# Output blocks of nine products laid over two pairs of steps in one order

## The chip, the cores and the metric

The kernel runs on one core of a Trainium2 chip. The metric is device time in microseconds (us) from start to end of one execution. Three runs of the kernel before gave 1628.75, 1627.30 and 1627.44 us; the median is 1627.44 us.

Engines are named as in the profile: PE (TensorE, matmuls; PEld are its weight loads), DVE (VectorE), ACT (ScalarE), POOL (GpSimd) and SP (SyncE, which issues most of the transfers; SPq is its queue).

## The reference, cut to what matters

```python
# xn = layernorm(x), x: 2048 tokens x 512
q, k, v = split(xn @ wqkv)                  # 32 heads of 16
p = softmax(q @ k.T / 4)                    # per head, 2048 x 2048
s = concat_heads(p @ v) @ wo
h = layernorm(xn)
u = gelu(h.T @ w1 + b1)                     # MLP over the tokens, F = 1792
y = (u @ w2 + b2).T
out = x + s * silu(y)
```

The output is 2048 x 512 in f32. Products that are not attention products are made of three matmuls each: operands are split into a high and a low part (h, l), and hh, hl and lh are summed.

## The kernel before, in words

Heads are worked in 16 pairs. For one pair of heads the kernel goes twice over the keys, once for each half of the queries (1024 rows, a "span"). One step `t` is one block of 128 keys against a span of queries, for both heads of a pair. It makes four score tiles of 128 x 512 (`score`, line 987: a matmul into a bank of PSUM named `sc`, then an exponential on ACT into a tile `prob`, line 992). Two steps later `values` (line 1003) multiplies the four tiles with the values and adds them up in a bank named `av`; this is eight matmul records, called an av set below.

The softmax needs the maximum of each row beforehand. So 22 steps (`LEAD`) ahead of the scores the same product is made the other way round for steps `u` (`max_of`, line 532, banks named `mx`), and DVE takes the maximum of each 128 x 512 tile (line 536). After 16 steps `max_rows` is called. It gives two parts, which are put in a list `pieces`: `first_` reduces the 16 steps' maxima and turns one block of 32 x 32, `last` turns three more blocks (line 548), and then POOL splits the result in two (lines 559 and 94) and issues four transfers on its own queue (line 98) that write it as two extra rows into the query tile of either head (first both rows of head a = 0, then both of a = 1). The scores of that span, six steps on, multiply 50 rows instead of 48 and so read these rows.

The loop over `s` goes by pairs of steps, from 0 to 534; steps s and s + 1 of the maxima run beside steps s - 22 and s - 21 of the scores and s - 24 and s - 23 of the av sets. One pair of steps holds 8 maxima, 8 scores and 2 av sets. Heads a = 0 and a = 1 sit in rows 0 to 63 and 64 to 127 of the PE array, so that two matmuls, one for each half, run beside each other: this is a slot. Into these slots goes other work (`Fill`, written D): products of the mixer MLP up to s = 456, and after that the output product, which `rest` makes in 14 blocks (`PARTS`) of nine products: three groups of eight heads times hh, lh, hl. Each product is cut into its upper and lower 64 rows, so a block is 18 half products. They add up in one bank that `hold` takes out of the four `sc` banks; while it is held the scores rotate over three.

`ORDERS` (line 1117) gives the order within one pair of steps. It has one string for each half of the PE array, and each letter is a maximum (m), a score (s) or a half product (D); the two numbers behind are the places at which an av set goes ahead of the slot. At the first of them `piece()` runs one of the waiting pieces; at both `run_later()` runs what has been put off (`after(n, f)` puts `f` off by n such calls). `halves` takes n products from the fill and `count` says how many: for a block of nine it gives 4 in the first pair of steps and 5 in the second. `lead`, the half of the array that has its D at the front of its string, changes after each pair. At the end of a pair the functions that end a block (`then`) are called: `part` copies the bank to a tile with ACT (line 910), the bank goes back, and POOL multiplies and adds (lines 913, 914) before SP stores (line 921).

When a span of a pair of heads is done, `put_away` copies the av bank out (line 723) and stores it. After the last pair of a group `invert` puts off a function `two`: DVE takes reciprocals of the row sums (line 751), and SP stores them to DRAM (line 752). `two` waits in `pieces` as well. At the start of a pair of steps `divisions` looks whether the reciprocals were stored, and `divide` then loads numerators and reciprocals (lines 775, 779). Later POOL multiplies (line 786), casts to the high part (line 798) and subtracts for the low part (line 94). The last of these divisions feeds the first block of the final stage (s >= 512, line 1188), of which the first two products need the high part and the third the low part.

Of the kernel before, what the change touches and what calls it, by code (L numbers as in the profile page):

```python
# [21 lines left out]
def tile_attention_token_mixer(ctx, tc, x, wqkv, wo, w1, b1, w2, b2, out):  # L22
    nc = tc.nc
    P = 128
    S, D = x.shape
# [11 lines left out]
    LEAD = 22  # L37
# [132 lines left out]
    with (  # L170
# [172 lines left out]
        two = first(0, range(2, 4), True)  # L343
# [64 lines left out]
        for c in range(NC):  # L408
# [20 lines left out]
            for n, (part, g) in enumerate(order):  # L429
                m = slice(g * P, (g + 1) * P)  # L430
# [75 lines left out]
    now = [0]  # L506
# [420 lines left out]
    def load_second():  # L927

        b = next((b for b in unkept if b >= PARTS), min(unkept))
        unkept.remove(b)  # L930
        i = b - NB // 2
        while not held or len(held) < NB // 8:
            held.append(big.tile([P, S], F32, name="big"))
        ys[b] = held[i // 4][:, i % 4 * 512 : i % 4 * 512 + 512]
        nc.sync.dma_start(ys[b], y_d[b] if b < PARTS else xv[:, b, :])
# [145 lines left out]
    def take(n, each):  # L1081

        nonlocal open_, done
        got = 0
        while open_ and (got < n or fill.peek() and len(fill.peek()) == 2):
            x = fill.next()
            if x is False:
                open_ = False
            elif x is None:
                break  # L1090
            elif len(x) == 2:
                def then(empty, back):
                    empty()
                    back()

                each(None, lambda x=x: then(*x))
                if fill.peek() is None:
                    fill.next()
                    break
            else:  # L1100
                each(x, None)
                got += 1
        done += got
# [98 lines left out]
    def items(s, a):  # L1202
# [7 lines left out]
                sc.append(lambda t=t, i=i, at=(ps_mx, "mx") if a and s >= NU else (ps_sc, "sc"): score(t, i % 2, a, *at))  # L1210
        return mx, sc

    take(FIRST, whole)
    after(5, lambda: load_v(0))
    if NP > 1:
# [4 lines left out]
    def piece():  # L1220
        if pieces:
            pieces.pop(0)()
            return True
        return False

    lead = 0
    for s in range(0, total + 1, 2):
        t = s - LEAD
        now[0] = s
        if s >= NU or t < 0:  # L1230
            run_later()
        if done >= n_fill // 2 + 3 * NF:
            divisions()
        if s >= NU - SPP + LEAD and unkept:
            load_second()
        if s == NU:

            ps_sc.free += ps_mx.free
            ps_mx.free = ps_sc.free
        heads = [items(s, a) for a in range(2)]  # L1240
        if s < NU and t >= 0:
            steady[0] = True
            one, two, then = halves(lead, count())
            made = [dict(D=part, m=heads[a][0], s=heads[a][1]) for part, a in ((one, lead), (two, 1 - lead))]
            first, second, *places = order(len(one), new_block[0])
            if one:
                lead = 1 - lead
            for i, kinds in enumerate((*zip(first, second), "")):
                if i in places:

                    if i == places[0]:
                        piece()
                    now[0] = s + places.index(i)
                    if now[0] >= LEAD + 2:
                        values(now[0] - LEAD - 2)
                    run_later()
                for of, kind in zip(made, kinds):
                    if of[kind]:
                        of[kind].pop(0)()
            for f in then:  # L1260
                f()
        elif s < NU:

            for i in range(4):
                for a in range(2):
                    max_of(s + i // 2, i % 2, a, *first_banks[n_max % 4])
                    n_max += 1
                end = i == 3 and s + 2 == LEAD
                some = []
                take(EARLY[n_max // 2 % len(EARLY)], lambda *x: some.append(x))  # L1270
                for x in some:
                    lanes(*x, stop=end and x is some[-1])
                if end:
                    keep_half()
                if i == 1:
                    now[0] = s + 1
                    run_later()
        else:


            for i in range(2):

                a_half(*(heads[a][1][2 * i : 2 * i + 2] for a in range(2)), i == 0 or s >= NU + 2 * (PARTS - NB // 2))
                if not piece() and asides and s < total - 2:
                    asides.pop(0)()
                for v in range(t - 2, t + i):
                    if (v, 0, 0) in prob:
                        values(v)
                if i == 0:
                    now[0] = s + 1  # L1290
                    run_later()
            if s == NU + 4:
                load_last_w()
            for _ in in_halves[:2]:
                load_half()
            if s == total - 6:
                split_last_w()
# [124 lines left out]
```

## Time and profile before

| | before |
|---|---|
| median of three runs | 1627.44 us (1627.30 to 1628.75) |
| the profiled execution's own time | 1627.72 us |
| its span, first to last instruction | 1625.8 us |
| granted clock of TensorE | 0.999 |
| PE busy | 1618.6 us (100%) |
| DVE busy | 1421.3 us (87%) |
| ACT busy | 1195.8 us (74%) |
| POOL busy | 559.9 us (34%) |
| the 14 output blocks | about 1402 to 1556 us of the span |

All times in the rows are microseconds from the first instruction of the span. In a row of the timeline stand the start, the length, the engine, the line, the operation, the tiles (written <- read), their shapes, the count of merged instructions, and in square brackets the idle time before it and who ended it. Matmul records overlap: a record of 0.39 us does not keep the next matmul on the same half of the array from starting 0.23 us after it. So starts are compared here, and the busy share of PE says little.

### The profile page before, as it was taken

To read this page: it belongs to the slowest core of one execution; us is meant where nothing else is said; L and a number is where in the kernel's file an instruction comes from. 1 tells how busy PE (TensorE), PEld (TensorE's weight loads), DVE (VectorE), ACT (ScalarE), POOL (GpSimd) and SP (SyncE) were. 2 spreads that over 40 slices of the span, in tenths; PEclk is the share of its full clock that TensorE was granted. 3 is DMA by queue.
4 is the path that set the end of the run, shared out by engine and by line. 5 is a ranking of instruction groups with operands and counts; after the bars stand their busy time and mean duration, and the time that the engine had idled before them with its cause. 6 is when DMAs were issued, how large, how long until landed. Compare 5 with 4: busy or idle time off the path is not lost.

```text
span 1625.8 us, 31245 instructions
## 1 busy us (share of the span) xinstructions
PE 1618.6 (100%) x11937; PEld 876.6 (54%) x11937; DVE 1421.3 (87%) x2492; ACT 1195.8 (74%) x2312; POOL 559.9 (34%) x665
## 2 busy tenths in 40 slices
PE   9999999999999999999999999999999999999998
PEld 7888854554555544544545545545545445444444
DVE  7665999999999999999999999999999999999956
ACT  3333477777777777778877877777777778888885
POOL 1224844342244432342333332322322233632440
PEclk9999999999999999999999999999999999999999
DMA  7478441514142141926151512314151615353365
GB/s 228 177 249 206 114 93 41 95 43 73 41 71 71 32 79 34 244 66 109 39 86 38 86 61 44 76 25 69 38 85 38 112 39 94 120 98 119 115 186 194
DMA packets 152466, 155.60 MB, mean 96 GB/s; under 512 B 51628, under 2 KB 110252, under 8 KB 149244
## 3 DMA queue, kind: packets, MB, share of 16 engines
q1 hardware_dynamic: 147900, 152.85, 38.6%
q8 instruction: 94, 1.54, 0.4%
q0 software_dynamic: 4416, 0.75, 0.4%
q14 instruction: 56, 0.46, 0.1%
HBM read 101.86 MB, written 50.58 MB: 94 GB/s over the span
## 4 chain that ended last, share of the span: by engine, by line
PE 99%; DMA 0%; DVE 0%; ACT 0%; SPq 0%; issue 0%; POOL 0%; DVEq 0%
PE av L1003 31%; PE dn L1144 24%; PE sc L987 16%; PE mx L532 15%; PE sc L435 3%; PE dn L670 3%; PE mx L435 2%; PE av L435 1%; PE sc L101 0%; PE sc L103 0%; PE sc L102 0%; PE mx L987 0%; DMA wl<-in_A_wqkv_dram 0%; PE mx L101 0%; PE mx L103 0%; PE mx L102 0%
## 5 line engine op out<-in xcount | busy, mean ns | idle before, releaser
L536 DVE TENSOR_REDUCE mxp<-mx 128x1 f32<-128x512 f32 x2026 | 1251.8, 682 | 118.3 <-PE mx L532 100.3
L992 ACT ACTIVATE prob<-sc 128x512 f32<-128x512 f32 x2004 | 1039.3, 607 | 284.6 <-PE mx L532 126.8
L532 PE MATMUL mx<-big 48*128 48x512 f32 x2026 | 773.7, 419 | 0.0
L987 PE MATMUL sc<-big 50*128 50x512 f32 x2004 | 739.8, 412 | 0.1
L1003 PE MATMUL av<-prob,vp 128*32 128x512 f32 x4096 | 545.5, 604 | 0.2 <-DVE ev L721 0.2
L1144 PE MATMUL dn<-hu,wh 64*128 64x512 f32 x1520 | 507.4, 404 | 0.0
L987 PEld LDWEIGHTS sc<-big 50*128 50x128 f32 x2004 | 354.2, 186 | 238.8 <-ACT prob L992 210.6
L532 PEld LDWEIGHTS mx<-big 48*128 48x128 f32 x2026 | 358.0, 185 | 195.4 <-DVE mxp L536 178.2
L1144 PEld LDWEIGHTS dn<-hu,wh 64*128 64x128 f32 x1520 | 271.9, 184 | 73.6 <-issue 49.5
L1144 PE MATMUL dn<-hu,wl 64*128 64x512 f32 x762 | 302.3, 397 | 0.0
L1003 PEld LDWEIGHTS av<-prob,vp 128*32 128x32 f32 x4096 | 80.9, 108 | 180.3 <-issue 168.0
L94 POOL TENSOR_TENSOR wl<-raw,wh 128x512 fp32r<-128x512 f32 x124 | 150.7, 1217 | 60.0 <-ACT wh L166 26.6
L1144 PEld LDWEIGHTS dn<-hu,wl 64*128 64x128 f32 x762 | 140.5, 184 | 12.1
L164 POOL CAST wh<-raw 128x512 fp32r<-128x512 f32 x104 | 60.4, 580 | 192.1 <-PE mx L532 79.5
L559 POOL CAST m<-f 16x128 fp32r<-16x128 f32 x32 | 9.0, 280 | 303.6 <-DVE f L548 303.6
L98 POOL DMA_DIRECT2D big<-m x128 | 66.2, 525 | 2.7 <-PE mx L987 2.7
L620 POOL TENSOR_TENSOR sq<-u 128x512 f32<-128x512 f32 x11 | 11.4, 1041 | 133.0 <-ACT u L614 132.9
L1144 PE MATMUL dn<-wh,hu 64*128 64x512 f32 x168 | 55.1, 393 | 0.0
L707 POOL TENSOR_SCALAR t<-t 128x512 f32<-128x512 f32 x16 | 23.8, 1488 | 83.7 <-ACT t L704 83.7
L435 PE MATMUL sc<-xt,big 128*128 128x512 f32 x184 | 44.3, 389 | 0.0
L94 POOL TENSOR_TENSOR hu<-hx,hu 128x512 fp32r<-128x512 f32 x16 | 20.4, 1292 | 68.4 <-ACT hu L278 68.4
L670 PE MATMUL dn<-hu,wh 64*128 64x512 f32 x128 | 42.3, 392 | 0.0
(233 smaller groups left out, 1212.1 us busy)
## 6 DMA issues: line engine op xcount, KB each, us to landing
raw<-in_B_w_dram SPq DMA_DIRECT2D x104, 256.0 KB
big<-k_d SPq DMA_DIRECT2D x96, 128.0 KB
big<-q_d SPq DMA_DIRECT2D x96, 128.0 KB
q_d<-sg SPq DMA_DIRECT2D x16, 512.0 KB
k_d<-sg SPq DMA_DIRECT2D x16, 512.0 KB
num_d<-ev SPq DMA_DIRECT2D x30, 256.0 KB
u_d<-uo SPq DMA_DIRECT2D x14, 512.0 KB
hu<-u_d SPq DMA_DIRECT2D x14, 512.0 KB
```

The lines of the kernel that those rows point to most:

```text
L94: eng.tensor_tensor(out=o, in0=a, in1=b.bitcast(F32), op=OP.subtract)
L98: queue.dma_start(dst.bitcast(F32), src.bitcast(F32))
L164: nc.gpsimd.tensor_copy(whs[n][:, :m, :], raws[n][:, :m, :])
L435: nc.tensor.matmul(ps, w[part][:, kd, m], xt[kd][:, z, :], start=w is wh and z == 0 and kd == 0, stop=w is wl and kd == ND - 1,)
L532: nc.tensor.matmul(ps, q[o : o + 48, r * P : (r + 1) * P], k[o : o + 48, c * 512 : (c + 1) * 512], start=True, stop=True,)
L536: nc.vector.tensor_reduce(mxp[u // 16][:, a, r % 8, c : c + 1], ps, axis=AX.X, op=OP.max)
L670: nc.tensor.matmul(ps, w(slice(0, 64)), m(slice(0, 64)), start=first, stop=last)
L707: nc.gpsimd.tensor_scalar(t, t, 1.0, None, op0=OP.add)
L987: nc.tensor.matmul(ps, ks[p][o : o + 50, kb * P : (kb + 1) * P], qs[p][o : o + 50, at : at + 512], start=True, stop=True,)
L992: nc.scalar.activation(e, ps, AF.Exp, scale=scale)
L1003: nc.tensor.matmul(av[32 * j : 32 * j + 32, :], vps[p][:, kb, 16 * a : 16 * a + 32], prob.pop((t, a, c)), start=kb == 0, stop=kb == NB - 1,)
L1144: made.append(lambda r=r, start=first and a == lead, stop=last and a != lead: nc.tensor.matmul(ps, w(r), m(r), start=start, stop=stop,))
```

## The change

A new table `WIDE` holds one order for a whole block of nine products, over two pairs of steps (25 slots, the same letters in number as before: 18 D, 16 m, 16 s). `both_pairs` emits it whenever a pair with s divisible by four starts a new block of nine; the loop's next pair then emits nothing but what stands behind the slots. This holds for all 14 blocks, s = 456, 460, ..., 508. The differences in what is emitted:

- Each half of the array has its nine D in one burst of its own: slots 3 to 11 on the half of `lead`, slots 15 to 23 on the other. `lead` no longer changes.
- The bank of the block is taken at slot 3 and given back at slot 23 (`then` is called behind the last D, not at the end of the pair).
- The four av sets stand ahead of slots 2, 12, 15 and 24, each followed by `run_later()`.
- `piece()` is called ahead of slots 12 and 24, where before it was called at the first av set of each pair.
- `keep` (divisions and loads) of the second pair is called ahead of slot 15.

```diff
+    WIDE = ("mssDDDDDDDDDsmsmsmmssmsmm", "smmsmsmsmsmsmmsDDDDDDDDDs", 2, 12, 15, 24)
+
+    def both_pairs(s, keep):
+
+        heads = [[x + y for x, y in zip(items(s, a), items(s + 2, a))] for a in (lead, 1 - lead)]
+        made = [dict(m=mx, s=sc) for mx, sc in heads]
+        first, second, *places = WIDE
+        one, two, then = [], [], []
+        for i, kinds in enumerate((*zip(first, second), "")):
+            if i in places:
+                n = places.index(i)
+                if n == 2:
+                    keep(s + 2)
+                if n % 2:
+                    piece()
+                now[0] = s + n
+                values(now[0] - LEAD - 2)
+                run_later()
+            if "D" in kinds and not one and not two:
+                one, two, then = halves(lead, 9)
+                assert len(one) == len(two) == 9
+            for of, rows, kind in zip(made, (one, two), kinds):
+                (rows if kind == "D" else of[kind]).pop(0)()
+            if then and not two:
+                then.pop()()
...
     for s in range(0, total + 1, 2):
         t = s - LEAD
-        now[0] = s
+        now[0] = max(s, now[0])
         if s >= NU or t < 0:
             run_later()
-        if done >= n_fill // 2 + 3 * NF:
-            divisions()
-        if s >= NU - SPP + LEAD and unkept:
-            load_second()
+        if s != second_pair:
+            keep(s)
...
         heads = [items(s, a) for a in range(2)]
-        if s < NU and t >= 0:
+        if s == second_pair:
+            pass
+        elif s < NU - 2 and s % 4 == 0 and done >= n_fill and count() == 4 and new_block[0]:
+            both_pairs(s, keep)
+            second_pair = s + 2
+        elif s < NU and t >= 0:
```

Three places of the order are shown. The first is PE where one output block ends and the next begins; `dn` is the block's bank (its number names the block), `wh`/`wl` and `hu` are operands of the output product, `sc` and `mx` are score and maximum. Before:

```order
L1144 MATMUL dn_20656<-wh_20154,hu_19919 128x512
L987 MATMUL sc_20816<-big_1481,big_1482 128x512
L1144 MATMUL dn_20656<-wl_20155,hu_19919 128x512
L532 MATMUL mx_20821<-big_1372,big_1371 128x512
L1144 MATMUL dn_20656<-wh_20154,hu_19919 128x512
L1144 MATMUL dn_20827<-wh_19981,hu_10896 128x512
L987 MATMUL sc_20829<-big_1481,big_1482 128x512
L1144 MATMUL dn_20827<-wl_19982,hu_10896 128x512
L532 MATMUL mx_20834<-big_1372,big_1371 128x512
```

PE at such a place after the change:

```order
L1144 MATMUL dn_20531<-wh_20154,hu_19919 128x512
L1003 MATMUL av_20333<-prob_20544,vp_18318 32x512
L1003 MATMUL av_20333<-prob_20553,vp_18318 32x512
L1003 MATMUL av_20333<-prob_20579,vp_18318 32x512
L1003 MATMUL av_20333<-prob_20592,vp_18318 32x512
L532 MATMUL mx_20649<-big_1372,big_1371 128x512
L987 MATMUL sc_20652<-big_1481,big_1482 128x512
L532 MATMUL mx_20658<-big_1372,big_1371 128x512
L987 MATMUL sc_20661<-big_1481,big_1482 128x512
```

Before, the next block's D follows the old block's last D in the same burst, so the next bank is taken at once; now an av set, three slots and another av set stand between.

The second place is DVE in blocks s = 496 to 508, from the last turned maxima (line 548) to the end of the stage; line 751 is the last reciprocal, `mxp` the maxima. Before:

```order
L548 STREAM_TRANSPOSE f<-neg_141 32x32 x3
L536 TENSOR_REDUCE mxp<-mx 128x1 x32
L751 RECIPROCAL d<-d 96x64
L536 TENSOR_REDUCE mxp<-mx 128x1 x22
L94 TENSOR_TENSOR hu<-sq,hu 96x512
```

DVE after the change:

```order
L548 STREAM_TRANSPOSE f<-neg_141 32x32 x3
L536 TENSOR_REDUCE mxp<-mx 128x1 x32
L751 RECIPROCAL d<-d 96x64
L536 TENSOR_REDUCE mxp<-mx 128x1 x17
L94 TENSOR_TENSOR hu<-sq,hu 96x512
```

The reciprocal, and the turned maxima 32 maxima before it, stand five maxima later in the program than before.

The third place is SP around the store and the load of these reciprocals (`rec_d`), with the stores of output blocks (`y_d`). Before:

```order
L752 DMA rec_d_1_135<-d 96x64
L775 DMA u<-num_d_1_127 96x1x512
L775 DMA sq<-num_d_1_127 96x1x512
L779 DMA uo<-rec_d_1_135 96x1x1024
L935 DMA big<-y_d 128x512
L921 DMA y_d<-t 128x512
```

SP after the change:

```order
L752 DMA rec_d_1_135<-d 96x64
L921 DMA y_d<-t 128x512
L775 DMA u<-num_d_1_127 96x1x512
L775 DMA sq<-num_d_1_127 96x1x512
L779 DMA uo<-rec_d_1_135 96x1x1024
L935 DMA big<-y_d 128x512 x2
```

One store of an output block now stands between the store of the reciprocals and the loads.

More of the change, by code (lines that the diff above doesn't have):

```diff
@@ L1226, in tile_attention_token_mixer, with keep @@
     lead = 0
-    for s in range(0, total + 1, 2):
-        t = s - LEAD
-        now[0] = s
-        if s >= NU or t < 0:
-            run_later()
+    second_pair = None
+    def keep(s):
         if done >= n_fill // 2 + 3 * NF:
@@ L1235, in tile_attention_token_mixer @@
             load_second()
+    for s in range(0, total + 1, 2):
+        t = s - LEAD
+        now[0] = max(s, now[0])
+        if s >= NU or t < 0:
+            run_later()
+        if s != second_pair:
+            keep(s)
         if s == NU:
```

## The prediction

> **What bounds the kernel now.** I read the page first, then the lines of the output blocks, then the timeline there, engine by engine.
>
> ```profile
> span 1625.8 us, 31245 instructions
> PE 99%; DMA 0%; DVE 0%; ACT 0%; SPq 0%; issue 0%; POOL 0%; DVEq 0%
> ```
>
> The chain that ended last is PE almost throughout, so a gap on PE counts in full and a gap elsewhere only where PE waits for it. The two lines of the output products say where the change acts:
>
> ```profile
> L1144 PE MATMUL dn<-wh,hu x168: 383/391/490, 1402.4 to 1556.4; 64*128 64x512 f32 x168
> L1144 PE MATMUL dn<-wl,hu x84: 386/393/501, 1402.9 to 1556.1; 64*128 64x512 f32 x84
> ```
>
> 252 half products are 14 blocks of 18, from 1402 to 1556 us, a tenth of the span. The same av set thirteen blocks apart (timeline of PE):
>
> ```profile
> 1409.60 1.07 PE L1003 MATMUL av<-prob,vp 128*32 128x512 f32 x8
> 1552.43 1.07 PE L1003 MATMUL av<-prob,vp 128*32 128x512 f32 x8
> ```
>
> 142.83 / 13 = 10.99 us a block. One block in the same view, reading starts only:
>
> ```profile
> 1449.03 0.49 PE L987 MATMUL sc<-big 50*128 50x512 f32 x1
> 1449.93 1.07 PE L1003 MATMUL av<-prob,vp 128*32 128x512 f32 x8
> 1450.92 0.49 PE L532 MATMUL mx<-big 48*128 48x512 f32 x1
> 1451.27 0.39 PE L1144 MATMUL dn<-wh,hu 64*128 64x512 f32 x1
> 1453.13 0.39 PE L1144 MATMUL dn<-wh,hu 64*128 64x512 f32 x1
> 1453.55 1.07 PE L1003 MATMUL av<-prob,vp 128*32 128x512 f32 x8
> ...
> 1456.45 0.49 PE L532 MATMUL mx<-big 48*128 48x512 f32 x1
> ...
> 1459.01 1.07 PE L1003 MATMUL av<-prob,vp 128*32 128x512 f32 x8
> ```
>
> The D at 1451.27 and 1453.13 are eight slots apart: 0.2325 us a slot. Three slots between av sets take 0.90 (1449.03 to 1449.93), which is 3 x 0.2325 + 0.20, so entering and leaving an av set costs 0.20. An av set is 1.0. Without waits ten slots would take 2.53 and nine 2.29; measured are 2.63 (1450.92 to 1453.55) and 2.56 (1456.45 to 1459.01). So 0.10 + 0.27 = 0.37 us of a block is waiting, and that is all that an order can win: 5.2 us over 14 blocks, 0.3% of the kernel. The nine-slot burst waits here (weight loads of PE, then ACT):
>
> ```profile
> 1457.87 0.18 PEld L987 LDWEIGHTS sc<-big 50*128 50x128 f32 x1 [0.19 <-ACT prob L992]
> 1458.35 0.18 PEld L987 LDWEIGHTS sc<-big 50*128 50x128 f32 x1 [0.19 <-ACT prob L992]
> 1457.21 1.09 ACT L992 ACTIVATE prob<-sc 128x512 f32<-128x512 f32 x2 [0.56 <-PE dn L1144]
> 1458.18 0.59 ACT L910 COPY t<-dn 128x512 f32<-128x512 f32 x1
> ```
>
> The old block's bank is being copied while the next block has already taken another, so scores rotate over two free banks. The exponentials begin at 1457.21 and 0.49 later, each 0.60 long; the two loads start just as these end. DVE is nearly as tight:
>
> ```profile
> 1449.60 4.94 DVE L536 TENSOR_REDUCE mxp<-mx 128x1 f32<-128x512 f32 x8 [0.51 <-PE mx L532]
> 1455.11 4.95 DVE L536 TENSOR_REDUCE mxp<-mx 128x1 f32<-128x512 f32 x8 [0.57 <-PE mx L532]
> ```
>
> Eight maxima take 4.9 of 5.5 us. DVE becomes the limit only below 9.9 us a block.
>
> **The steady block.** Slots, av sets, exponentials, maxima and copies are the same in number, as are stretches between av sets (3, 10, 3 and 9 slots). Only waits can change. I count from the start of the av set ahead of slot 24: slots 24, 0, 1 at 1.00, 1.33, 1.56; av set at 1.89; slots 2, 3, 5, 7, 9, 11 at 2.89, 3.22, 3.69, 4.15, 4.62, 5.09; then 5.42 av set, 6.41 to 6.98 slots 12 to 14, 7.31 av set, 8.31 to 10.27 slots 15 to 23, and 10.6 the next av set. The copy of the finished bank now runs at 0.6 to 1.1, while ACT would idle, and the bank is back before slot 3 takes another. Scores stand at slots 2, 3, 5, 7, 9 and 11; their exponentials begin at 3.42 (0.53 after a score behind an av set) and then every 0.48, as those of the score at 1449.03 and its next two do:
>
> ```profile
> 1449.56 1.57 ACT L992 ACTIVATE prob<-sc 128x512 f32<-128x512 f32 x3 [0.76 <-PE mx L532]
> ```
>
>  With three banks, slot 7 needs slot 2's (free 4.02), slot 9 slot 3's (4.51), slot 11 slot 5's (4.99): each 0.10 to 0.13 ahead of its slot, where a load of 0.18 would like some 0.15. I take 0.07 a block for these and for the maxima, whose three banks come free by the same small margin at slots 10 and 23. So 0.30 of the 0.37 goes: 13 blocks, -3.9 us. Bounds: 0, and -4.8 (no wait left).
>
> **Start.** In block 456 ACT still has work of the mixer:
>
> ```profile
> 1401.15 0.49 PE L532 MATMUL mx<-big 48*128 48x512 f32 x1
> 1404.09 1.07 PE L1003 MATMUL av<-prob,vp 128*32 128x512 f32 x8
> 1402.29 1.09 ACT L992 ACTIVATE prob<-sc 128x512 f32<-128x512 f32 x2
> 1405.82 3.78 ACT L992 ACTIVATE prob<-sc 128x512 f32<-128x512 f32 x7
> ```
>
> Before, this burst of nine lasts 2.94, that is 0.65 of waiting, and the next 0.10. ACT's order up to 1405.82 stays. After, slot 1 needs the first of the two exponentials from 1402.29 (+0.3), and slot 2's score, made at about 1404.4, is exponentiated at 1405.82 only; slot 7, due at 1405.6, waits for that bank until 1406.5 (+0.9). Net 1.2 - 0.75 = +0.5 (0 to +1.2). In block 460 a cast (line 798) falls ahead of slot 2's exponential: +0.15.
>
> **Turned maxima.** Three times in the stage `last` goes out, now ahead of slot 24 instead of five maxima earlier, and the next block's slot 9 is already the first score that needs its rows (head 0, `lead` being 1); slot 16 needs the other head's. The chain (DVE, POOL, and the landing of line 98's four transfers):
>
> ```profile
> 1476.68 0.63 DVE L548 STREAM_TRANSPOSE f<-neg 32x32 f32<-32x32 f32 x3
> 1478.13 2.04 POOL L98 DMA_DIRECT2D big<-m  x4
> DMA to landing us min/median/max: 1.6/1.6/1.6
> ```
>
> From the end of the transposes (1477.31) 0.82 to the first issue, 0.51 to the second, 1.6 to land: 2.95. DVE works off three buffered maxima first, to 1.3, and ends the transposes at 1.95; so the rows are there at 4.9, and slot 9 is due at 4.62. POOL has nothing queued ahead at that moment. With the load's start: +0.45 each (0 if DVE is not behind, 1.5 if it takes the third and fourth transfer too), three times +1.35. DVE being 0.6 late delays slots 6 and 8 by less than that.
>
> **End of the stage.** The last block leads into the final stage:
>
> ```profile
> 1555.32 0.50 PE L532 MATMUL mx<-big 48*128 48x512 f32 x1
> 1558.36 0.64 PE L1003 MATMUL av<-prob,vp 128*32 128x512 f32 x4
> ```
>
> Ten slots in 3.04 instead of 2.53: an av set stands behind the burst now and gives ACT its time, -0.5.
>
> **The last division.** This is the term that turns the sum. Its reciprocals wait in the same `pieces`, so they move from the first av set of pair 506 to slot 24 of block 504, seven slots and an av set later. The products that need the result move by nothing. The rows in the order of the chain (DVE, SP, POOL, PE):
>
> ```profile
> 1542.49 0.55 DVE L751 RECIPROCAL d<-d 96x64 f32<-96x64 f32 x1
> 1543.06 0.32 SPq L752 DMA_DIRECT2D rec_d<-d  x1
> 1545.11 0.69 SPq L779 DMA_DIRECT2D uo<-rec_d  x1
> 1546.35 0.41 SPq L921 DMA_DIRECT2D y_d<-t  x1
> 1552.90 1.28 POOL L786 TENSOR_TENSOR u<-u,uo 96x512 f32<-96x512 f32 x1 [3.49 <-DMA uo<-rec_d]
> 1555.36 0.61 POOL L798 CAST hu<-u 96x512 fp32r<-96x512 f32 x1
> 1556.05 1.29 POOL L94 TENSOR_TENSOR hu<-u,hu 96x512 fp32r<-96x512 f32 x1
> 1557.56 0.40 PE L1188 MATMUL dn<-wh,hu 64*128 64x512 f32 x1
> 1558.03 0.39 PE L1188 MATMUL dn<-wh,hu 64*128 64x512 f32 x1
> ```
>
> From the reciprocal's start the high part is ready after 13.48 (1555.97), the low part after 14.85 (1557.34). The first product came at 1557.56 and the third at 1558.03, so the cover is 1.6 and 0.7 us. Counted from block 504's last av set, the reciprocal now starts at 1.33, behind the buffered maxima; block 508's last av set is at 10.70, then 1.0, slot 24 and two slots with scores alone: the first product is due at 12.50, the third at 12.97. One store more in SP's queue ahead (0.4 as in the row of line 921) makes the high part 15.2 and the low part 16.6. PE stands 2.7 and in all 3.6, with the load's start 3.7 us. Behind it on PE are the two av sets of step 512, on ACT the cast of the other 512 columns and the scores' exponentials; nothing there makes it up, as PE bounds that stage too. The unknown is the load's 7.79 us from issue to POOL. Lower end: it lands like the tiny transfers in 1.6, no stall. Upper end: the 6.2 between are shared by the three loads it stands among, 2.1 each, and the store adds as much: 5.8. I take the measured 7.79, since queue, sizes and neighbours stay.
>
> The Trainium skill, "DMA: Bandwidth & Descriptors", section "Anatomy of one DMA — SWDGE (gpsimd) path", fits a transfer's time as 2.0 us plus its bytes over 436 GB/s, for another queue than SP's. For 96 rows of 4 KB this is an estimate of 2.9 us, 4.9 less than the row; by it the high part would be there at 10.3 and the low part at 11.7, ahead of 12.5, and the sum would lose the 3.7: the first rival below. The trace of this load disagrees.
>
> **Sum.** -3.9 + 0.5 + 0.15 + 1.35 - 0.5 + 3.7 = +1.3 us on the profiled execution's 1627.72 (its span and 1.9 us around it). The median of the runs is 0.3 below that: 1627.44 + 1.3 = 1628.7.
>
> **Rivals.**
> - The last load comes in time, since fewer transfers crowd it when it is issued later: no stall at the end, 1628.7 - 3.7 = 1625.0. For it: its packets waited among two other loads. Against: those are issued with it again.
> - That, and the turned maxima in time too, because DVE is less behind than I count: 1625.0 - 1.35 = 1623.6, faster. It decides once load and rows together cost under 0.6 us. Against it: DVE's idle time is only 0.51 and 0.57 a pair.
> - The bursts wait as before, because all margins are about 0.1 us and one cast on ACT is 0.5: no gain in the blocks, 1628.7 + 3.9 = 1632.6, slower by 0.3%. It decides when a block wins less than 0.15. For it: block 460 as worked out above.
>
> **How the numbers follow.** No measurement of this kernel tells less than about 0.2% (3.25 us) from no change. Forecast 0.47 (1626.5 to 1630.7), first rival 0.15, second 0.13, third 0.25. Faster is the second, 0.13; slower the third, 0.25; within 0.2% the rest, 0.62. The range 1624.5 to 1632.0 leaves out the second rival and the far end of the third. The likeliest case's own range is 1626.5 to 1630.7.
>
> **What would show it.** The block should be 10.7 us between like av sets, with no ACT wait in the nine-slot burst; a wait of slot 9 for `big<-m` three times; line 786's last wait ending about 12.2 after block 504's last av set; PE idle some 3 us ahead of the first product of line 1188. I am wrong if blocks stay at 11.0, or if line 1188 starts without waiting.

## The result, and the profile after

The changed kernel takes 1632.64 us (median of seven runs, 1631.10 to 1633.66) against 1627.44 us before (seven runs, 1627.08 to 1628.75): a ratio of 1.0031, 95% interval 1.0019 to 1.0043. It is slower by 5.2 us, and 0.6 us beyond the upper end of the predicted range. The profiled execution's own time is 1633.66 us. A profile shows one execution of a kernel; where that execution lies more than 0.5 us off the kernel's median, its own time is given below.

The page after, the span and the chain of work that ended last:

```profile
span 1631.8 us, 31244 instructions
PE 92%; DVE 3%; DMA 2%; ACT 1%; POOL 1%; SPq 0%; issue 0%; DVEq 0%; POOLq 0%
```

Before, the chain was PE by 99%. Now it leaves PE, and one of the lines that it goes through is the load of the reciprocals (`uo<-rec_d`, 1% of the span). To see where, I take the output stage between two like av sets, before (timeline of PE):

```profile
1400.16 1.06 PE L1003 MATMUL av<-prob,vp 128*32 128x512 f32 x8
...
1558.36 1.92 PE L1003 MATMUL av<-prob,vp 128*32 128x512 f32 x16
1560.89 1.07 PE L1003 MATMUL av<-prob,vp 128*32 128x512 f32 x8
```

and after, the same two av sets, with one whole block (1459.16 to 1469.83) between them:

```profile
1400.86 1.07 PE L1003 MATMUL av<-prob,vp 128*32 128x512 f32 x8
...
1459.16 1.07 PE L1003 MATMUL av<-prob,vp 128*32 128x512 f32 x8
...
1462.73 1.06 PE L1003 MATMUL av<-prob,vp 128*32 128x512 f32 x8
...
1464.63 1.06 PE L1003 MATMUL av<-prob,vp 128*32 128x512 f32 x8
...
1467.93 1.06 PE L1003 MATMUL av<-prob,vp 128*32 128x512 f32 x8
...
1469.83 1.06 PE L1003 MATMUL av<-prob,vp 128*32 128x512 f32 x8
...
1562.29 3.64 PE L1003 MATMUL av<-prob,vp 128*32 128x512 f32 x16
1566.94 1.06 PE L1003 MATMUL av<-prob,vp 128*32 128x512 f32 x8
```

From the first row to the last it is 160.73 us before and 166.08 after: 5.35 us come from this stage. (The other 0.6 us between the two profiled executions are there before the stage begins: 1400.16 against 1400.86.) The block is shorter, as forecast: 10.67 us instead of 10.99. Its nine-slot burst (nine slots between two av sets) takes 3.30 less an av set of 1.00, so 2.30 instead of 2.56, and its ten-slot burst 2.57. All of the loss lies at the stage's end. The chain there, after, in the order of DVE, SP, POOL and PE:

```profile
1545.12 0.55 DVE L751 RECIPROCAL d<-d 96x64 f32<-96x64 f32 x1
...
1548.21 0.69 SPq L779 DMA_DIRECT2D uo<-rec_d  x1
...
1557.12 1.26 POOL L786 TENSOR_TENSOR u<-u,uo 96x512 f32<-96x512 f32 x1 [9.39 <-DMA uo<-rec_d]
1559.55 0.61 POOL L798 CAST hu<-u 96x512 fp32r<-96x512 f32 x1
1560.21 0.79 PE L1188 MATMUL dn<-wh,hu 64*128 64x512 f32 x1 [3.74 <-POOL hu L798]
1560.23 1.28 POOL L94 TENSOR_TENSOR hu<-u,hu 96x512 fp32r<-96x512 f32 x1
1560.80 0.62 PE L1188 MATMUL dn<-wl,hu 64*128 64x512 f32 x1
1561.57 0.29 PEld L1188 LDWEIGHTS dn<-wh,hu 64*128 64x128 f32 x1 [0.86 <-POOL hu L94]
```

PE stands 3.74 us for the high part, and its third product then waits once more for the low part: the stall that the prediction describes. What it does not describe is the length of the records: the first product of line 1188 takes 0.79 instead of 0.40, and the 16 matmuls of the two av sets behind it 3.64 instead of 1.92. The busy times by stretches show why (the column after the five engines is TensorE's granted clock):

```profile
1557.00:1558.00 1.00, 0.00 (x0) 0.00 (x0) 0.00 (x0) 0.00 (x0) 0.88 (x1) 1.00 0.40 152
...
1560.00:1561.00 1.00, 0.79 (x3) 0.50 (x3) 0.72 (x1) 1.00 (x3) 0.92 (x2) 0.50 0.02 6
...
1564.00:1566.00 2.00, 2.00 (x14) 0.34 (x6) 0.00 (x0) 0.00 (x0) 1.92 (x2) 0.50 0.17 26
1566.00:1568.00 2.00, 2.00 (x14) 0.58 (x14) 0.00 (x0) 1.31 (x3) 0.77 (x3) 0.80 1.01 289
```

The clock falls to 0.50 about 0.2 us before PE starts again, and stays there for 6.83 us (1559.98 to 1566.80 in the record of the clock). Before, it is 1.00 through this whole part.

The account of the stage: 3.74 us of waiting; from the first product of line 1188 to the av sets 2.08 instead of 0.80 before (1557.56 to 1558.36), so 1.28; from there to the next av set 4.65 instead of 2.53 (1558.36 to 1560.89), so 2.12. That is 7.1 us of loss at the end, and 5.35 - 7.1 = -1.8 us for everything ahead of it. The 1.28 is not clock alone: the third product starts only when POOL has made the low part.

### The profile page after: what moved, and what is told of

It reads as the page before. It is cut to its first block, busy times and chain, and to the rows that moved or that the text cites. A ratio compares the mean times of both kernels' runs of the same rounds, so it can differ in the third digit from the quotient of the medians.

```text
span 1631.8 us, 31244 instructions
## 1 busy us (share of the span) xinstructions
PE 1620.4 (99%) x11937; PEld 877.8 (54%) x11937; DVE 1422.2 (87%) x2492; ACT 1197.7 (73%) x2312; POOL 559.8 (34%) x665
## 4 chain that ended last, share of the span: by engine, by line
PE 92%; DVE 3%; DMA 2%; ACT 1%; POOL 1%; SPq 0%; issue 0%; DVEq 0%; POOLq 0%
PE av L1003 31%; PE dn L1144 24%; PE sc L987 16%; PE mx L532 14%; PE dn L670 2%; PE sc L435 1%; PE mx L435 1%; DMA xr<-in_A_x_dram 1%; DVE st L225 1%; PE dn L671 1%; DVE mxp L536 1%; DMA uo<-rec_d 1%; DVE sg L94 1%; ACT prob L992 1%; PE dn L1188 0%
## 5 line engine op out<-in xcount | busy, mean ns | idle before, releaser
L1144 PE MATMUL dn<-wh,hu 64*128 64x512 f32 x168 | 58.5, 401 | 0.0
```

Source lines behind the costliest of these rows:

```text
L1144: made.append(lambda r=r, start=first and a == lead, stop=last and a != lead: nc.tensor.matmul(ps, w(r), m(r), start=start, stop=stop,))
```

## The experiments

All ratios are to the kernel before, measured beside each kernel on the same chip. Its medians there were 1626.54 us (late division alone, 40 unread products, division at slot 12, bank kept), 1627.14 us (the four from division at slot 15 to 15 unread products), 1626.12 us (the next three) and 1626.95 us (the last one). A turn is one call of `piece()`, the place where a waiting piece may run; unread products are products whose result nothing uses.

| kernel | median, us | ratio, 95% interval |
|---|---|---|
| late division alone, on the kernel before | 1630.86 | 1.0028 (1.0016 to 1.0039) |
| changed, division at slot 15 of block 504 | 1627.91 | 1.0006 (0.9997 to 1.0015) |
| changed, all turns at slots 2 and 15 | 1631.31 | 1.0018 (1.0009 to 1.0027) |
| changed, only the maxima at slots 2 and 15 | 1633.80 | 1.0037 (1.0023 to 1.0051) |
| changed, 15 unread products on half the array | 1632.82 | 1.0032 (1.0020 to 1.0043) |
| changed, 40 unread products on both halves | 1629.97 | 1.0020 (1.0010 to 1.0030) |
| changed, division at slot 12 of block 504 | 1628.44 | 1.0010 (1.0001 to 1.0019) |
| that, bank kept into the next block | 1637.25 | 1.0064 (1.0049 to 1.0080) |
| division at slot 12, last rows off POOL | 1625.36 | 0.9995 (0.9986 to 1.0004) |
| before, last rows off POOL | 1626.40 | 1.0001 (0.9992 to 1.0010) |
| division at slot 12, last rows and both low rows off POOL | 1628.00 | 1.0013 (1.0004 to 1.0022) |
| division at slot 12, last rows and one low row off POOL | 1624.69 | 0.9985 (0.9976 to 0.9994) |

**Is it the late division?** First the division alone, put into the kernel before:

```diff
-                    if i == places[0]:
+                    if i == places[0] and s != NU - 6:
                         piece()
...
+                if s == NU - 6 and i == 12:
+                    piece()
                 for of, kind in zip(made, kinds):
```

> The kernel before, with only the last reciprocals moved: to the end of pair 506, where 17 maxima are left behind them on DVE, as in the changed kernel (before: 22). Theory A (late result, idle PE, then a lower clock): PE waits 1.5 to 3.0 us ahead of line 1188, the clock falls to 0.5 for 3.4 or 6.8 us, and the time is 1627.4 + 3.5 to 6.5 = 1631 to 1634. Theory B (the idle time alone, as forecast): 1629.0 to 1630.5 and the clock at 1.0.

The ratio of 1.0028 is 4.3 to 4.6 us, inside what the first theory gives and above the second's. The timeline of PE and the stretches (this execution took 1631.99 us):

```profile
1559.35 0.49 PE L1188 MATMUL dn<-wh,hu 64*128 64x512 f32 x1 [1.99 <-POOL hu L798]
...
1560.70 0.63 PE L1188 MATMUL dn<-wh,hu 64*128 64x512 f32 x1 [0.64 <-POOL hu L94]
...
1561.28 3.41 PE L1003 MATMUL av<-prob,vp 128*32 128x512 f32 x16
```

```profile
1558.00:1559.00 1.00, 0.00 (x0) 0.00 (x0) 0.00 (x0) 0.23 (x1) 1.00 (x2) 1.00 0.57 141
...
1561.00:1562.00 1.00, 1.00 (x6) 0.20 (x8) 0.93 (x6) 0.54 (x1) 1.00 (x2) 0.50 0.35 117
```

2.6 us of waiting, then the clock at 0.50 for 3.41 us. So the loss comes from one moved `piece`, without any of the new order, and it is larger than the waiting.

**The division taken back ahead of time.** One more turn at slot 15 of block 504:

```diff
-                if n % 2:
+                if n % 2 or n == 2 and s == NU - 8:
                     piece()
```

> Only the turn of the last reciprocals moves, in block 504 from slot 24 to slot 15; the turned maxima stay late. Theory A: 1632.6 - 5.9 = 1626.7 us, granted clock 1.0 throughout the final stage, slot 9 still waits for the rows three times. Theory B: 1629.5 us.

Measured: 1627.91 us, between the two numbers. In the profiled execution (1628.65 us) PE's waits shrink to 0.30 and 0.62 us, but the clock still falls to 0.50, for 3.41 us (1557.81 to 1561.22). So most of the loss is gone with the waiting, and a rest stays with the clock.

**Other places for the turns.** All turns at slots 2 and 15, and then only the maxima there while the division stays late:

```diff
-                if n % 2:
+                if n % 2 == 0:
                     piece()
```

> The waiting pieces run ahead of slots 2 and 15 (first and third av set of a block) and no longer ahead of slots 12 and 24; all else as after the change. Theory A (the last division comes late, PE idles 3.7 us, and its clock then drops to half for some 6 us, together 7.3 us; the turned maxima cost 0.45 us three times): the reciprocals start about 3.1 us earlier, PE idles under 2 us, no drop of the clock, no wait for the rows: 1632.6 - 5.9 - 1.4 = 1625.3 us. Theory B (only the wait counts, the half clock is without effect on the end): 1632.6 - 3.1 - 1.4 = 1628.1 us.

```diff
-                if n % 2:
+                if n % 2 == (s % 16 != 0):
                     piece()
```

> Only the turned maxima move, to slots 2 and 15 of their block; the reciprocals stay at slot 24 of block 504. Both theories: the three ten-slot bursts of 3.0 us fall to 2.6, 1632.6 - 1.3 = 1631.3 us, and the clock drops in the final stage as before. If the late rows were the main loss it would fall to 1628 or below.

Both miss upwards: 1631.31 and 1633.80 us. The first one's profiled execution (1628.90 us) shows what I had not reckoned with, three blocks with two slow bursts each; why most of its other executions took some 2.5 us more, no profile shows. One of the blocks (DVE's and PE's rows):

```profile
1432.75 0.63 DVE L548 STREAM_TRANSPOSE f<-neg 32x32 f32<-32x32 f32 x3
...
1434.00 0.18 PEld L532 LDWEIGHTS mx<-big 48*128 48x128 f32 x1 [0.61 <-DVE mxp L536]
...
1434.60 0.18 PEld L532 LDWEIGHTS mx<-big 48*128 48x128 f32 x1 [0.30 <-DVE mxp L536]
```

The transposes stand between maxima while all three `mx` banks are full, and PE waits for a bank; the nine-slot burst takes 2.87 instead of 2.31, and the ten-slot burst ahead of it 2.97. At slots 12 and 24 the same transposes fall into a gap of DVE. By these bursts the places that the change chose for the maxima are the better ones, although slot 9 waits there; the times (1.0037 against 1.0031) do not tell the two apart. The division is what suffers from these places.

**What lets the clock fall?** If it is PE standing idle, work in place of the idle time should keep the clock. First on rows 0 to 47 alone:

```diff
         if s == NU:
+            idle = ps_mx.tile([P, 512], F32, name="mx")
+            for i in range(15):
+                nc.tensor.matmul(idle, ks[NP - 1][:48, :P], ks[NP - 1][:48, :512], start=True, stop=True)
```

> As after the change, but 15 matmuls whose result nobody reads (48 x 512, about 3.5 us in all) stand on PE where it waits for the last division, ahead of the two scores. The wait itself stays. Theory A: the clock stays at 1.0, the av sets behind take 0.85 to 1.0 us and not 1.7, 1632.6 - 2.8 = 1629.8 us. Theory B: no gain, 1632.6 us or more.

Measured: 1632.82 us. In the profiled execution (1632.02 us) PE stands 0.74 and 0.54 us instead of 3.74 and 0.15, and the clock falls all the same, to 0.50 for 6.83 us (1558.73 to 1565.56). So the theory fell in this form. Then the same with both halves of the array, and long enough to cover all of the waiting:

```diff
         if s == NU:
+            idle = [ps_mx.tile([P, 512], F32, name="mx") for a in range(2)]
+            for i in range(40):
+                r = slice(64 * (i % 2), 64 * (i % 2) + 48)
+                nc.tensor.matmul(idle[i % 2], ks[NP - 1][r, :P], ks[NP - 1][r, :512], start=True, stop=True)
```

> The changed kernel with 40 products that nobody reads at the start of step 512, 20 on rows 0 to 47 and 20 on rows 64 to 111 in turn, some 4.65 us in place of the 3.74 us in which PE stands idle. Theory A (PE's idle time, with a half-used array counting as half idle, is what lets the clock fall): the clock stays 1.0, the products behind are as fast as before the change, and the time is about 1632.6 + 0.9 - 3.6 = 1629.9. Theory B (the fall does not depend on how busy PE is): 0.5 again for 3.4 or 6.8 us, and the time is 1632.5 to 1633.6.

Measured: 1629.97 us, where 1629.9 was expected; against the kernel before beside it that is 3.4 us, where 2.5 were expected (0.54 of it is a wait at 1571.8 us for the rows of the last maxima, which comes up again below). The same two views:

```profile
1559.73 0.49 PE L1188 MATMUL dn<-wh,hu 64*128 64x512 f32 x1 [0.25 <-POOL hu L94]
...
1560.16 1.92 PE L1003 MATMUL av<-prob,vp 128*32 128x512 f32 x16
```

```profile
1560.00:1562.00 2.00, 2.00 (x18) 0.42 (x16) 1.16 (x6) 0.95 (x2) 1.92 (x3) 1.00 0.00 0
```

The division is as late as in the changed kernel, PE computes 4.6 us of nothing, and yet the kernel is faster than the changed one, because the clock stays at 1.00 and the 16 matmuls take 1.92 instead of 3.64. Nor is this one profile alone: over the whole span the mean granted clock is 0.998 in all seven executions of the changed kernel and 0.999 or 1.000 in all eight of this one. How much rest is enough to lose the clock is not settled. In this part of the kernel it fell in each profile with 2.3 us and more of waiting; in two profiles after shorter waits (0.30 and 0.62 us; 0.74 and 0.54 us); and not in the one with a single wait of 0.63 us (all turns at slots 2 and 15), nor here after 0.25 and, 12 us later, 0.54 us, nor in any profile with shorter waits alone. The two kernels with unread products differ in the rows used and also in the waits that were left, so which of the two kept the clock is open.

The Trainium skill, "TensorE: Matmul & The Clock Gate", section "Part 1: The HAM clock gate", says that a block of the chip judges how busy PE was in free-running windows of 4096 cycles, 3.4 us, and gates the clock to half after an idle one. The lengths here agree: 3.41 us or twice that in every fall. The advice of the Trainium skill, "TensorE: Matmul & The Clock Gate", section "Why this matters for your kernels", to have no idle gaps of PE above about 3 us does not hold as a limit here, since the clock fell after gaps of 0.3 and 0.6 us as well.

**Is it the bank that made the blocks shorter?** With the division at slot 12 (below) as the base, the finished bank is copied only at slot 6 of the next block:

```diff
+            if i == 6 and waiting:
+                waiting.pop()()
             if then and not two:
-                then.pop()()
+                waiting.append(then.pop())
+        if s == NU - 4:
+            waiting.pop()()
```

> The kernel with the reciprocals at slot 12 (same call), but each block's finished bank is copied out only at slot 6 of the next block instead of right after its last product, so that two banks are held at the start of each block. Theory A (the blocks got shorter because the bank comes back before the next block takes one): the bursts wait for ACT again, by 0.25 to 0.3 us a block or more, 12 blocks, so 1625.3 + 3.3 = 1628.6 or above. Theory B (it is the order of slots that saves the waiting): bursts at 2.31 and 2.58 as in the changed kernel, 1625.3.

Measured: 1637.25 us, 8.8 more than its base, against 3.3 or more expected. In the two profiles 7.5 us of it lie in the output stage (166.76 against 159.26 between the same two av sets); the rest comes behind it, where the clock falls for 6.83 us instead of 3.41. The ten-slot burst goes from 2.6 to about 3.27 in the regular blocks; the nine-slot burst stays at 2.31. One ten-slot burst (PE's weight loads and ACT's copy of the old bank):

```profile
1472.44 0.18 PEld L987 LDWEIGHTS sc<-big 50*128 50x128 f32 x1 [0.42 <-ACT prob L992]
...
1473.47 0.58 ACT L910 COPY t<-dn 128x512 f32<-128x512 f32 x1
1473.62 0.18 PEld L987 LDWEIGHTS sc<-big 50*128 50x128 f32 x1 [0.40 <-ACT prob L992]
...
1474.10 0.18 PEld L987 LDWEIGHTS sc<-big 50*128 50x128 f32 x1 [0.18 <-ACT t L910]
```

So the moment at which the old bank is copied and comes back is worth more than the whole gain of the blocks. The edit moves both at once, the copy into a stretch where ACT is busy and the bank's return behind it, so which of the two costs more is not shown. That the order of the slots adds to it was not tried apart.

**The division at slot 12.** There DVE has its gap and a turn stands free in block 504; the reciprocals come due one turn sooner:

```diff
-        after(8 if g < ND - 1 else 2, lambda: pieces.append(two))
+        after(8 if g < ND - 1 else 2 - span, lambda: pieces.append(two))
```

> The changed kernel, but the last division's reciprocals become due one turn earlier: slot 12 of block 504 instead of slot 24, two av sets and 13 slots (5.3 us) sooner; maxima keep their turns at slots 12 and 24. Theory A (the late division and the half clock behind it cost some 7.3 us, all the rest is as forecast): line 1188 starts with a wait under 0.3 us, the clock stays 1.0 to the end, the turned maxima still cost 3 x 0.46, and the time is 1632.6 - 7.3 = 1625.3, ratio 0.9987. Theory B (the tail only shows what the order costs anyway, or the clock falls whenever the stage ends): the idle time goes, but the clock still falls to 0.5 for 3.4 us or more and the time is 1627.5 to 1629.5, as when the reciprocals went out at slot 15.

Measured: 1628.44 us, not 1625.3. The wait ahead of the first product of line 1188 is gone (the weight load of the third still waits 0.32 us for the low part), and up to the av set behind it the stage takes 159.26 us (1398.99 to 1558.25), 1.47 less than before. But 9 us further on PE stands again (POOL, then PE, then the landing of line 98's transfers, then the stretches of the profiled execution, 1628.94 us):

```profile
1565.30 2.05 POOL L98 DMA_DIRECT2D big<-m  x4 [2.70 <-PE dn L1188]
...
1569.83 0.18 PEld L987 LDWEIGHTS sc<-big 50*128 50x128 f32 x1 [3.40 <-DMA big<-m]
1569.86 0.46 PE L987 MATMUL sc<-big 50*128 50x512 f32 x1 [2.52 <-DMA big<-m]
```

```profile
DMA to landing us min/median/max: 3.2/3.7/4.3
```

```profile
1572.00:1573.00 1.00, 1.00 (x10) 0.13 (x2) 0.33 (x1) 0.43 (x1) 0.00 (x0) 0.50 0.91 258
```

The rows of the last maxima come too late for the scores that read them, and 1.6 us after PE goes on, the clock falls for 3.41 us. The timeline of the kernel before at the same place (POOL, then PE's weight loads):

```profile
1565.40 2.04 POOL L98 DMA_DIRECT2D big<-m  x4 [2.70 <-PE mx L987]
...
1569.92 0.18 PEld L987 LDWEIGHTS sc<-big 50*128 50x128 f32 x1 [0.84 <-DMA big<-m]
```

There too the rows were what that weight load waited for last; 0.84 is the usual gap of weight loads behind an av set, so PE lost nothing, but the rows had little to spare: the second transfer, issued at 1565.95, landed 3.8 us later, about 0.2 us ahead of that weight load. They are made by POOL, at the end of a queue that is busy without a pause from line 786 to line 94: division, memsets, gating of a block (lines 913, 914), then the cast and the split of the rows. From line 786 to the first transfer it is 12.5 us before (1552.90 to 1565.40) and 12.4 after (1557.12 to 1569.56). So, with POOL's queue ending when it did, a shorter stage could not have made the kernel faster by more than about 0.2 us: PE would have come to this wait instead. In the kernel with the division at slot 12, POOL's queue also holds one operation more. The low part of the other 512 columns is made on POOL while `now[0]` is below 512 and on DVE from there on (`eng`), and the earlier division takes it from DVE (before, first row) to POOL (division at slot 12, second row):

```profile
1558.18 0.69 DVE L94 TENSOR_TENSOR hu<-sq,hu 96x512 fp32r<-96x512 f32 x1 [0.45 <-ACT hu L798]
```

```profile
1556.34 1.30 POOL L94 TENSOR_TENSOR hu<-sq,hu 96x512 fp32r<-96x512 f32 x1
```

It holds the next operation of that queue back by 1.36 us (1556.34 to 1557.70), so by this estimate about half of the 2.52 us of waiting comes with it; a kernel that leaves it on DVE was not run.

**The last rows off POOL.** For the last span alone DVE, which is idle then, does the cast and the split, and SP the four transfers:

```diff
-            nc.gpsimd.tensor_copy(m[:, 0, :], f[:16, :])
-            sub(nc.gpsimd, m[:, 1, :], f[:16, :], m[:, 0, :])
+            by, queue = (nc.vector, nc.sync) if u // 16 == NU // 16 - 1 else (nc.gpsimd, nc.gpsimd)
+            by.tensor_copy(m[:, 0, :], f[:16, :])
+            sub(by, m[:, 1, :], f[:16, :], m[:, 0, :])
...
-                        m[8 * a : 8 * a + 8, t, :], nc.gpsimd,
+                        m[8 * a : 8 * a + 8, t, :], queue,
```

> The kernel with the reciprocals at slot 12 of block 504, and beside that the last four rows of maxima are cast and split on DVE and stored through SP's queue, where POOL does both in all other stretches. Theory A (POOL's queue at the stage's end is what took the gain back: its rows were issued at 1565.30 in both the kernel before and the one with the early reciprocals, so that PE, 2.6 us earlier, waited for them until 1569.86): the rows land by about 1563.7, the score that needs them starts without a wait, and the stage's gain of some 1.5 us reaches the end: 0.9991 of the kernel before, and the clock falls in few executions or none. Theory B (something else holds PE there, or the loads behind the four stores on SP now come late): PE waits again ahead of that score or of its neighbours, and the ratio is 1.0000 or above.

> The kernel before, with the last four rows of maxima cast and split on DVE and stored through SP's queue. Theory A (before, the rows land 0.9 us ahead of their score, so nothing waits for them): the same time as before, ratio 0.9997 to 1.0003. Theory B (the detour over POOL costs something in the kernel before too): 1626 us or less against 1627.4, ratio below 0.9993.

On top of the early division: 1625.36 us, 0.9995, between the two theories' 0.9991 and 1.0000. On the kernel before: 1.0001, so by itself it does nothing, as expected. With both, the timeline of SP and the stretches show the rows issued from 1560.97 on and PE without a gap there:

```profile
1560.97 2.84 SPq L98 DMA_DIRECT2D big<-m  x4
```

```profile
1566.00:1568.00 2.00, 2.00 (x18) 0.59 (x16) 0.33 (x1) 2.00 (x5) 1.71 (x4) 1.00 0.94 317
```

The stage takes 159.76 us (1399.07 to 1558.83), 0.97 less than before and not 1.5, since its last nine-slot burst takes 2.75 instead of 2.31. The kernel is 0.36% below the changed one, if both ratios to the kernel before are set against each other, and the interval against the kernel before still holds 1.

**The turned maxima.** The rows of a turn, in the changed kernel (POOL's issue and the weight load of slot 9, then the landing of these transfers):

```profile
1481.40 2.04 POOL L98 DMA_DIRECT2D big<-m  x4
...
1483.67 0.18 PEld L987 LDWEIGHTS sc<-big 50*128 50x128 f32 x1 [0.49 <-ACT prob L992]
```

```profile
DMA to landing us min/median/max: 1.6/1.6/1.6
```

The wait is put down to ACT, but the exponential whose bank this score takes had ended 0.55 us earlier (1483.12). The second of the four transfers, issued at about 1481.9, lands at 1483.6. In the other two turns the wait is 0.45 and 0.43. To test it, the second rows of both heads, and then of the first head alone, go through SP's queue beside POOL's:

```diff
-                        m[8 * a : 8 * a + 8, t, :], queue,
+                        m[8 * a : 8 * a + 8, t, :], nc.sync if t and u >= NU - 64 else queue,
```

> The kernel with early reciprocals and the last rows off POOL (same call), and in the three turns of maxima within the blocks each head's second row goes through SP's queue instead of POOL's, so that it is issued beside the first and not 0.51 us behind it. Theory A (slot 9 waits 0.46 us for the second of four transfers): the ten-slot bursts of these three blocks last 2.6 instead of 3.04, and the time is 1.2 to 1.4 us below that of the other kernel, ratio 0.9982. Theory B (slot 9 waits for a bank that DVE or ACT holds, or SP's queue is blocked then): these bursts stay at 2.9 or above, and the time is the same as the other's or longer.

```diff
-                        m[8 * a : 8 * a + 8, t, :], nc.sync if t and u >= NU - 64 else queue,
+                        m[8 * a : 8 * a + 8, t, :], nc.sync if t > a and u >= NU - 64 else queue,
```

> The kernel with early reciprocals and the last rows off POOL, and in the three turns of maxima only the first head's second row goes through SP's queue (three transfers fewer on POOL, where the run with both heads' had six fewer). In the run with six fewer the three bursts fell to 2.78 to 2.84 and the last product of PE came 1.5 us earlier, but POOL's closing drain lasted 11.70 us instead of 2.31 and ended the span. Theory A (the long drain comes with moving these rows off POOL at all): the drain again lasts some 11 us and the time is 1627.5 to 1628.5. Theory B (it depends on what is left in POOL's queue): a drain of about 2.3 us, bursts of 2.8, and 1625.36 - 0.8 = 1624.6 us, ratio 0.9990.

In the first, the wait is

```profile
1437.91 0.18 PEld L987 LDWEIGHTS sc<-big 50*128 50x128 f32 x1 [0.21 <-ACT prob L992]
```

and the three bursts last 2.78, 2.84 and 2.81 instead of 3.06, 3.11 and 3.04. So the transfer was what slot 9 waited for, and about half of the 0.46 goes, not all. PE's last product comes 1.5 us earlier than without this. But the kernel is slower, 1628.00 us: its last store is issued by 1619.8, and the span ends at 1626.1, 6.3 us later, where the kernel before takes 2.5 (1623.3 to 1625.8). In the trace POOL's closing drain lasts from 1613.65 to 1625.35, 11.70 us, where it takes 2.31 without this edit. With one row only, the bursts are 2.82, 2.82 and 2.79, the drain takes 2.06 us, and the time is 1624.69 us, 0.9985 (0.9976 to 0.9994; the profiled execution took 1625.41 us). This is the lowest ratio of all, below the kernel before by 0.15% and below the changed one by about 0.46%; against 0.9995 without the moved row it is not told apart, as the two intervals overlap. What the long drain waited for, no run shows; it does not come with every row that leaves POOL's queue.

## Why the prediction was wrong

The forecast of 1628.7 us failed in one term of its sum, **the last division**, put at +3.7 us. It cost 7.1.

- The mechanism was right: the reciprocals went out at 1.35 us behind block 504's last av set (1543.77; forecast 1.33), the load was late, and PE stood ahead of the first product and again ahead of the third.
- The size of the wait was a little low. Line 786 waited until 13.3 us behind that av set, forecast 12.2. The load took 8.91 us from issue to POOL instead of the 7.79 that I took over, so PE stood 3.74 us for the first product instead of 2.7. In the terms of the forecast, the third product was due 12.97 us behind that av set and started 17.80 behind it, so the waiting cost 4.8 where 3.7 was put (counted by due times, which gives 7.3 for the whole loss; the account above counts from the end of PE's last record). The upper bound of 5.8 covered this.
- The step that failed is what comes behind the wait: "Behind it on PE are the two av sets of step 512 ... nothing there makes it up" priced it at no further loss. But it cost: half the clock for 6.83 us, 2.1 us in the av sets alone, and some 0.4 between the third product and them. No term, no rival and no bound had a stall of PE that makes the work behind it slower. The unread products show this step apart: same late result, 0.25 us of idle time there, full clock, and 1.8 us less than the changed kernel by the two ratios. On the kernel before, the late division alone cost 4.3 to 4.6 us, although PE waited only 2.6.

The other terms, in the order of the sum:

- **The steady block**, -3.9: right in kind. The nine-slot burst lost its wait (2.30 instead of 2.56); the block is 10.67 to 10.74 where 10.7 was forecast. Thirteen blocks, the turned maxima and block 460 with them, take 140.69 us (1408.61 to 1549.30, the av sets ahead of slot 12) instead of 142.83; without those two terms that is -3.6. The early copy and release of the bank is the cause, as far as tried: moving both back cost 7.5 us in the stage.
- **Start**, +0.5: the first seven slots took 2.31 and the ten behind them 3.45, 1.4 us of waiting against 0.75 before, so +0.65. **Block 460**, +0.15: its ten-slot burst is 2.78 against 2.58 to 2.65 in the regular blocks, so +0.13 to +0.20, as forecast.
- **Turned maxima**, +1.35: 0.49, 0.45 and 0.43 at slot 9, together 1.37, and by the mechanism named.
- **The end of the stage**, -0.5: not seen apart here, as the stall lies on it. With the division at slot 12 the six slots ahead of the av sets of step 512 still take 2.15 us, where six slots without waits would take 1.60 by the forecast's own prices: a score there waits for ACT (0.21) and the third product for POOL (0.32). Together the terms ahead of the division came to -1.8 us, forecast -2.4.

The rivals: the load did not land in time, so the first two did not come about. But the first one's number, 1625.0, was wrong for its own case too. With the division in time the kernel took 1628.44 us, because POOL's last rows held PE next (with one operation more ahead of them), and the row that showed their small reserve stood in the profile before. The third rival's time, 1632.6, is the measured one only by chance: it had the blocks without a gain, and they did gain.

## What to carry to other kernels

When a step is moved, follow its result to the consumer on the bounding engine, and price a stall there twice: the waiting, and the slower clock behind it. When a stage gets shorter, ask next which chain on another engine does not get shorter with it and ends just in time now; here it was POOL's queue, and only with both off the path, and one row of maxima on another queue, did the new order pay (0.9985). See also whether a choice of engine hangs on the step at which a piece runs: here the earlier division moved a subtraction from DVE to POOL, into the queue that was to be the next limit. Moving one `piece` by a slot is not free either: a DVE step costs nothing in DVE's gap and half a microsecond where all banks are full.

## What the runs showed of the hardware that I had not expected

- TensorE's clock falls to 0.50 for 3.41 or 6.83 us after one short rest, once even after two waits of 0.30 and 0.62 us. Products on half of the array's rows, 3.58 us of them in place of the idle time and with waits of 0.74 and 0.54 us left, did not keep it; products on both halves, with a wait of 0.25 us left, did.
- In the changed kernel the same four transfers of line 98 take 1.6 us from issue to landing within the blocks and 3.2 to 4.3 us at the stage's end.
- There POOL also starts the first of them 2.70 us after the split that it needs, in each profile that has it on POOL; within the blocks the first issue follows at once. What it waits for, no run shows.
- POOL's closing drain took 11.70 us in one kernel and 2.06 to 2.65 us in the others, and ended that kernel's span.
